# A rebuilt opening for an FFT mixing and MoE kernel: another scratch layout, fewer transfers, later weights

## The chip, the cores and the metric

One core of one Trainium2 chip runs the whole kernel. The time is device time in microseconds (us); a kernel's time is the median of its runs. Engines: PE is TensorE (matmuls; PEld its weight loads), DVE is VectorE, ACT is ScalarE, POOL is GpSimd, SP is SyncE, whose queue (SPq) issues every DMA of this kernel. PEclk is the granted TensorE clock as a share of 2.4 GHz; 0.50 is its other level, 1.2 GHz.

## The reference

```python
X = np.fft.rfft(x, axis=1)                     # x: 8 x 3008 x 256, f32
Yr = Xr @ w_r - Xi @ w_i + b_r
Yi = Xr @ w_i + Xi @ w_r + b_i
Yr, Yi = soft_threshold(Yr, 0.01), soft_threshold(Yi, 0.01)
y = np.fft.irfft(Yr + 1j * Yi, n=3008, axis=1)
out = (np.maximum(y @ w_in, 0) ** 2) @ w_out   # w_in 256 x 2048, w_out 2048 x 256, both f64
```

## The kernel before

The Fourier transform of length 3008 = 47 x 64 is done in two stages each way. Stage A transforms over 47 points, stage B over 64; then come the mix with `w_r` and `w_i`, bias and threshold, stage C (back over 64) and stage D (back over 47). Between the stages the data go through scratch in HBM: `scr1` from A to B, `scr2` from C to D. Frequencies come in 24 rows, worked on as 12 pairs for each batch. Most matmuls take an operand as a high and a low part (`split`, `mm3`: three matmuls for one product).

**The opening** (`start`, an order written out by hand) does all of batch 0 up to the first chunk of tokens, stage A of batch 1, and the weights. `loads` issues the input of batch 0 (`x0`) and the mixing weights. `stage_a(0)` is sixteen matmuls with `tU`, an eviction each (`copy`, in turn on ACT and DVE) and a store into `scr1`. Four weights begin during it, and `tables_start` builds the mixing tables. Then come fifteen rounds over `n`. Round n loads pair n+3 (`bin`) and two pieces of batch 1 (`x1`), does `pair_z(n-2)`, `pair_b(n)` (psb), `pair_mix(n-1)` (psm; the bias comes in as two matmuls of one row, high and low, against `one`), `pair_c(n-3)` and `pair_out` (psc, store to `scr2`), one step of stage A of batch 1 (psa, in rounds 2 to 13), `pair_turn(n-2)`, and one step of every weight under way (`weights`). A weight comes as f64: a load of 0.5 MB into one of four `w64` buffers, `narrow` to f32 (one pass on ACT, four on DVE), a high part by ACT, a low part by GpSimd; for `w_out` four more GpSimd operations on 128 columns. There are eight pieces of `w_in` and eight of `w_out`. After the rounds come `inverse` (loads of `din`, psd, then copy, unfold, high and low of three pieces in turn), the rest of stage A of batch 1, the rest of the weights and `tables_main`.

**The main loop** has 376 rounds of `mm1` (12 matmuls of 512 columns, `ph`), `squares`, `sums`, the split of `g` into `gh` and `gl`, and `mm2` (21 matmuls of 256 columns, `po`), three rounds behind. Stages A to D of the other batches are laid between these by a planner: each job has a round, a place in it and noted costs on ACT and DVE (`PAIR_WORK`, `A_WORK`, `D_WORK`), and `spread` picks the rounds in which these pile up least. `pair_rounds` fixes the pairs' rounds: batch 1 in 1, 3, ... 23. Stage A of batch 2 may begin at round 3. Each engine and each queue works in the order in which its instructions were issued. The first DMA of the loop is a load of `bin`.

Of the kernel before, what the change touches and what calls it, by code (L numbers as in the profile page):

```python
# [75 lines left out]
def tables():  # L76
# [47 lines left out]
    tb0 = tb.reshape(N2 // 4, 2, 2, 2, NR + 1, N2).transpose(0, 2, 3, 1, 4, 5).reshape(P, NR + 1, N2)  # L124
# [25 lines left out]
def fft_mix_moe(ctx: ExitStack, tc: tile.TileContext, xp, xu, w_r, w_i, b_r, b_i,  # L150
# [137 lines left out]

    def start():

        with ExitStack() as own:
# [12 lines left out]
            row = tl("t", name="row")[:1]
            rows = [tl(f"row{k}", (1, 2 * D), F32R) for k in range(2)]
            ones = tl("z", name="ones")[:1, :P]
            one = tMs[:1, 0, :]
# [40 lines left out]
            def tables_start():  # L348
# [8 lines left out]
                split(row, *rows)  # L357
# [15 lines left out]

            def narrow(t, h):


                lo, hi = t[:, :, 0], t[:, :, 1]
                hu = h.bitcast(U32)
                nc.scalar.activation(h, hi.bitcast(F32), AF.Abs)
                yield  # L380
                nc.vector.tensor_scalar(h, h, F_MIN, F_MAX, op0=ALU.max, op1=ALU.min)
                nc.vector.tensor_scalar(hu, hu, 5, 2, op0=ALU.logical_shift_left,
                                        op1=ALU.logical_shift_right)
                nc.vector.scalar_tensor_tensor(hu, lo, 29, hu,
                                               op0=ALU.logical_shift_right, op1=ALU.bitwise_or)
                nc.vector.scalar_tensor_tensor(hu, hi, 0xC0000000, hu,
                                               op0=ALU.bitwise_and, op1=ALU.bitwise_or)
# [23 lines left out]
            def win(c, k):  # L411
                def use(h):
# [5 lines left out]
                    nc.gpsimd.tensor_sub(wi_[1][:, k, s], h, wi_[0][:, k, s].bitcast(F32))  # L418
# [3 lines left out]
            def wout(j):  # L422
                def use(h):
# [9 lines left out]
                    for k in range(2):  # L433
# [3 lines left out]
                    (nc.gpsimd if j < 8 else nc.vector).tensor_sub(wo_[1][j], w7, wo_[0][j].bitcast(F32))  # L437
# [4 lines left out]
                                      (wout(j) for j in range(NU)))  # L442
# [570 lines left out]
```

## Time and profile before

| | us |
|---|---|
| median of 3 runs | 2577.48 |
| lowest and highest | 2576.4, 2577.53 |
| the profiled execution: its own time | 2579.61 |
| its span | 2577.8 |
| TensorE busy in it | 2511.0 (97%) |
| VectorE, ScalarE, GpSimd busy | 2104.9, 1989.6, 48.1 |

The span runs from the first instruction to the last. All of GpSimd's work lies in the first 150 us. Busy time is an average over stages with different limits, so the rows below look at single stretches.

### The profile page before, as it was taken

How to read it: one execution, taken by the hardware profiler on the slowest of the kernel's cores; microseconds unless marked ns; L12 is line 12 of the kernel's file. 1: busy time of each engine (PE TensorE's matmuls, PEld its weight loads, DVE VectorE, ACT ScalarE, POOL GpSimd, SP SyncE). 2: the span in 40 equal slices, each digit the busy share in tenths (PEclk: the TensorE clock that was granted, in tenths of full speed). 3: DMA queues.
4: the chain of work that ended last, by engine and by line, in shares of the span. 5: the costliest groups of instructions: out<-in, count | busy, mean ns of one | idle time of the engine just before them, and what ended most of it. 6: DMA issues, size and time to landing. Idle time of an engine off the chain costs nothing.

```text
span 2577.8 us, 42198 instructions
## 1 busy us (share of the span) xinstructions
PE 2511.0 (97%) x16627; PEld 2262.0 (88%) x16627; DVE 2104.9 (82%) x3155; ACT 1989.6 (77%) x2764; POOL 48.1 (2%) x57
## 2 busy tenths in 40 slices
PE   6979999999999999999999999999999999999999
PEld 3569999999999888999889998899988898899998
DVE  5868888888888888888888888888887888777777
ACT  3668887888788777878877888778877777777776
POOL 1410000000000000000000000000000000000000
PEclk8989999999999999999999999999999999999999
DMA  8622122221221112111122112121121111100000
GB/s 256 187 77 65 49 73 67 79 61 61 80 68 53 56 56 77 56 57 53 56 80 64 53 57 65 60 68 61 45 74 51 41 38 57 36 28 29 21 24 17
DMA packets 113095, 164.61 MB, mean 64 GB/s; under 512 B 9584, under 2 KB 63074, under 8 KB 112706
## 3 DMA queue, kind: packets, MB, share of 16 engines
q1 hardware_dynamic: 112898, 161.91, 20.5%
q8 instruction: 132, 2.16, 0.4%
q14 instruction: 65, 0.53, 0.1%
HBM read 86.90 MB, written 74.97 MB: 63 GB/s over the span
## 4 chain that ended last, share of the span: by engine, by line
PE 80%; DVE 8%; ACT 7%; DMA 3%; issue 2%; SPq 0%; DVEq 0%; ACTq 0%
PE po L906 20%; PE ph L185 10%; PE ph L184 10%; PE ph L186 10%; PE po L910 10%; PE psb L221 3%; PE psd L270 3%; PE psm L184 2%; PE psm L186 2%; PE psm L185 2%; DVE gl L951 2%; ACT g L891 2%; DMA din<-s 1%; ACT gh L946 1%; PE ph L882 1%
## 5 line engine op out<-in xcount | busy, mean ns | idle before, releaser
L951 DVE TENSOR_TENSOR gl<-g,gh 128x1792 fp32r<-128x1792 f32 x376 | 760.2, 2022 | 32.9 <-ACT gh L946 24.5
L891 ACT ACTIVATE g<-ph 128x512 f32<-128x512 f32 x752 | 408.4, 596 | 436.2 <-PE ph L186 305.9
L906 PE MATMUL po<-gh,wo 128*128 128x256 f32 x5264 | 683.8, 281 | 3.1 <-DVE o L923 2.2
L946 ACT CAST gh<-g 128x1792 fp32r<-128x1792 f32 x376 | 637.0, 1694 | 19.8 <-PE po L906 17.2
L906 PEld LDWEIGHTS po<-gh,wo 128*128 128x128 f32 x5264 | 633.3, 188 | 6.5 <-DVE o L923 6.0
L184 PE MATMUL ph<-xt,wi 128*128 128x512 f32 x1373 | 539.0, 393 | 11.9 <-DVE dx L278 9.4
L185 PE MATMUL ph<-xt,wi 128*128 128x512 f32 x1373 | 538.2, 392 | 0.0
L186 PE MATMUL ph<-xt,wi 128*128 128x512 f32 x1373 | 538.1, 392 | 0.0
L897 DVE TENSOR_TENSOR g<-g 128x512 f32<-128x512 f32 x376 | 259.8, 691 | 308.5 <-ACT g L892 306.7
L892 ACT ACTIVATE g<-g 128x1024 f32<-128x1024 f32 x376 | 399.4, 1062 | 12.0
L910 PE MATMUL po<-gl,wo 128*128 128x256 f32 x2632 | 360.5, 277 | 0.0
L910 PEld LDWEIGHTS po<-gl,wo 128*128 128x128 f32 x2632 | 326.8, 188 | 0.0
L184 PEld LDWEIGHTS ph<-xt,wi 128*128 128x128 f32 x1373 | 258.4, 188 | 58.4 <-ACT xt L282 9.5
L186 PEld LDWEIGHTS ph<-xt,wi 128*128 128x128 f32 x1373 | 258.4, 188 | 55.8
L185 PEld LDWEIGHTS ph<-xt,wi 128*128 128x128 f32 x1373 | 258.4, 188 | 44.3
L899 DVE TENSOR_TENSOR g<-g 128x256 f32<-128x256 f32 x376 | 160.0, 425 | 12.9
L898 DVE TENSOR_TENSOR g<-g 128x256 f32<-128x256 f32 x376 | 159.8, 425 | 12.9
L184 PE MATMUL psm<-wm,xh 128*128 128x256 f32 (+1 forms) x552 | 160.9, 291 | 4.4 <-DVE dx L278 3.7
L186 PE MATMUL psm<-wm,xl 128*128 128x256 f32 (+1 forms) x552 | 159.0, 288 | 0.0
L185 PE MATMUL psm<-wm,xh 128*128 128x256 f32 (+1 forms) x552 | 158.9, 288 | 0.0
L221 PEld LDWEIGHTS psb<-tB,bin 128*128 128x128 f32 x768 | 100.6, 194 | 39.0 <-issue 18.5
L270 PEld LDWEIGHTS psd<-tD,din 120*128 120x128 f32 (+1 forms) x832 | 107.2, 191 | 21.8 <-DMA din<-s 11.1
(108 smaller groups left out, 2822.7 us busy)
## 6 DMA issues: line engine op xcount, KB each, us to landing
bin<-s SPq DMA_DIRECT2D x96, 256.0 KB
s<-evc SPq DMA_DIRECT2D x96, 256.0 KB
outT_dram<-o SPq DMA_DIRECT2D x94, 256.0 KB
din<-s SPq DMA_DIRECT2D x96, 240.0 KB
xin<-in_xp_dram SPq DMA_DIRECT2D x72, 240.0 KB
s<-eva SPq DMA_DIRECT2D x72, 240.0 KB
s<-eva SPq DMA_DIRECT2D x22, 192.0 KB
w<-in_moe_w_in_dram SPq DMA_DIRECT2D x8, 512.0 KB
```

Of the source, the lines that this page charges most:

```text
L184: nc.tensor.matmul(out, l0, r0, start=start, stop=False, **kw)
L185: nc.tensor.matmul(out, l0, r1, start=False, stop=False, **kw)
L186: nc.tensor.matmul(out, l1, r0, start=False, stop=stop, **kw)
L221: nc.tensor.matmul(ps[:, k, :, q, :], tv[:, q, k], tB[:, 0:r + 2:r + 1], start=True, stop=True)
L270: nc.tensor.matmul(ps[:, k, part], t[:n, s:s + P], tD[:n, tab + part, :n], start=True, stop=True)
L891: nc.scalar.activation(g[:, 2 * a:2 * a + 2], ph[:, a].rearrange("p (t m) -> p t m", t=2), AF.Relu)
L892: nc.scalar.activation(g[:, 0:4], g[:, 0:4], AF.Square)
L897: nc.vector.tensor_sub(g[:, 4:6], g[:, 1:4:2], g[:, 0:2])
L906: nc.tensor.matmul(out, wo_[k][j][:, s], gh[:, s], start=j == 0 and half == 0 and k == 0, stop=False, skip_group_check=True)
L910: nc.tensor.matmul(out, wo_[0][j][:, s], gl[:, s], start=False, stop=j == NU - 1, skip_group_check=True)
L946: nc.scalar.copy(split_[r - 1][0], hid[r - 1])
L951: nc.vector.tensor_sub(gl, hid.pop(r - 1), gh.bitcast(F32))
```

## The change

- `scr1` is written in another order: one store per step, 48 rows of 4 KB, for both batches of the opening (before, 24 rows in one store for batch 0, two stores for batch 1). The table `t_b0` is permuted to match and serves batch 1 too; `t_b` is loaded into `tB` in the main loop, two rounds after batch 1's last pair.
- `w_r` and `w_i` come as one array and one DMA per half, the two biases as one row pair on partitions 0 and 32. The bias is one matmul over 33 partitions instead of two.
- `x0` is loaded ahead of the mixing weights, in six DMAs instead of seven; no weight begins during stage A of batch 0. Two begin after it and one in each of rounds 0 to 10, thirteen in all. `tables_start` comes after stage A.
- The last three of `w_out` (5, 6, 7) are done in main loop rounds 0, 2 and 5 (`plan_w`), with their four GpSimd operations each.
- Low parts of the weights go from GpSimd to DVE. Evictions of stage C and most of stage A of batch 1 go to ACT.
- Stage A of batch 1 begins at round 7 instead of 2; seven steps are left behind the rounds instead of four, and four of these use the `bin` buffers.
- Matmuls whose result is not used (`idle`): nine before the pairs, two before `inverse`'s matmuls, three after them.
- `inverse` does the three pieces interleaved instead of one by one.
- Main loop: batch 1's pairs in rounds 7, 9, ... 29; stage A of batch 2 from round 12; `e` and `t` of the threshold are one tile `et`, which `plan_w` uses too.

```diff
+LATE = ((5, 0), (6, 2), (7, 5))
-    tb0 = tb.reshape(N2 // 4, 2, 2, 2, NR + 1, N2).transpose(0, 2, 3, 1, 4, 5).reshape(P, NR + 1, N2)
+    tb0 = tb.reshape(N2 // 4, 2, 2, 2, NR + 1, N2).transpose(2, 0, 3, 1, 4, 5).reshape(P, NR + 1, N2)
-    out = {1: [1 + 2 * i for i in range(NPAIR)]}
+    out = {1: [7 + 2 * i for i in range(NPAIR)]}
...
-                load_x0(0, ((0, 2), (2, 4), (4, 8), (8, 12), (12, 16)))
+                load_x0(0, ((0, 2), (2, 4), (4, 8), (8, 16)))
+                load_x0(1, ((0, 8), (8, 16)))
                 for k in range(2):
-                    dma(out=raw[k][:, 1], in_=w_r[k * P:k * P + P, :])
-                    dma(out=raw[k][:, 2], in_=w_i[k * P:k * P + P, :])
-                load_x0(1, ((0, 8), (8, 16)))
-                dma(out=row[:, :D], in_=b_r[None, :])
-                dma(out=row[:, D:], in_=b_i[None, :])
+                    dma(out=raw[k][:, 1:3], in_=w_ri[k * P:k * P + P])
+                dma(out=row, in_=b_ri)
...
-                    nc.gpsimd.tensor_sub(wi_[1][:, k, s], h, wi_[0][:, k, s].bitcast(F32))
+                    (nc.gpsimd if WIL[2 * c + k] else nc.vector).tensor_sub(wi_[1][:, k, s], h, wi_[0][:, k, s].bitcast(F32))
...
-                    (nc.gpsimd if j < 8 else nc.vector).tensor_sub(wo_[1][j], w7, wo_[0][j].bitcast(F32))
+                    (nc.gpsimd if WOL[j] else nc.vector).tensor_sub(wo_[1][j], w7, wo_[0][j].bitcast(F32))
...
-                v = scr1[b].rearrange("r n (c d) -> r (n c) d", c=2)
+                v = scr1[b].rearrange("r n e -> (r n e)").rearrange("(p i e) -> p i e", p=2 * NR, i=nq)
...
-                    tag, n = ("ev", 3) if b else (("bin", 4), ("ev", 3), ("bin", 4), ("ld", 3))[i % 4]
+                    tag, n = (("ev", 3) if i < 12 else ("bin", 4)) if b else (("bin", 4), ("ev", 3), ("bin", 4), ("ld", 3))[i % 4]
                     e = tl(tag, bufs=n, name="eva")[:4 * NR]
-                    copy(i, e, o)
-                    if b == 0:
-                        v0 = scr1[b].rearrange("r n e -> r (n e)")[:, 4 * i * 2 * D:4 * (i + 1) * 2 * D]
-                        nc.sync.dma_start(out=v0.rearrange("r (m e) -> r m e", m=4), in_=e)
-                    for k in range(2 * b):
-                        q = 8 * i + 4 * k
-                        nc.sync.dma_start(out=v[:, q:q + 4], in_=e[:, k * D:k * D + D])
+                    copy(i if b == 0 else EV1[i], e, o)
+                    nc.sync.dma_start(out=v[:, i].rearrange("p (w e) -> p w e", w=2), in_=e)
...
-                for n in range(2):
-                    nc.tensor.matmul(p, one, rows[n], start=n == 0, stop=False)
+                nc.tensor.matmul(p, one, rows, start=True, stop=False)
...
+                for i, t in zip(first, got):
+                    ps[i] = points_d(i, t, pst("psd"))
+                for _ in range(WARM3):
+                    idle()
+                take(first[0])
+                unfold(first[0], ps[first[0]], v[first[0]], xf[first[0]])
+                for i, after in zip(first, first[1:] + [None]):
+                    if after is not None:
+                        take(after)
+                    high_x(pieces(i)[0], xf[i])
+                    if after is not None:
+                        unfold(after, ps[after], v[after], xf[after])
+                    low_x(pieces(i)[0], xf[i])
+
+            TAIL = 2
+            WARM = 9
+            WARM2 = 2
+            WARM3 = 3
+            EV1 = [0] * 10 + [0, 1] * 3
+            EVC = [0] * 12
+            WOL = [0] * 8
+            WIL = [0] * 8
+            X1 = 2, 2, 2, 2, 2, 2, 2, 2, 0, 0, 0, 0, 0, 0, 0
+            A1 = 0, 0, 0, 0, 0, 0, 0, 1, 1, 1, 1, 1, 1, 2, 1
+            WT = 1, 1, 1, 1, 1, 1, 1, 1, 1, 1, 1, 0, 0, 0, 0
...
-                if i == 9:
-                    tables_start()
-                if i in (9,11,13,15):
-                    weights()
-            for i in range(3):
-                load_pair(i)
+            tables_start()
+            load_pair(0)
+            load_pair(1)
             more_loads()
+            load_pair(2)
+            weights()
             weights()
+
+            def idle():
+                nc.tensor.matmul(pst("idle")[:4 * NR], tU, busy, start=True, stop=True)
...
+            for _ in range(WARM):
+                idle()
...
-            nc.sync.dma_start(out=tB, in_=t_b)
-            nc.sync.dma_start(out=bias2[:, 0, :], in_=b_r.partition_broadcast(P))
-            nc.sync.dma_start(out=bias2[:, 1, :], in_=b_i.partition_broadcast(P))
+            nc.sync.dma_start(out=bias2.rearrange("p c e -> p (c e)"), in_=b_ri[0].partition_broadcast(P))
...
+    W_WORK = ((0, .7, 2.3), (1, .8, .8), (2, .6, .7))
...
-            s["e"] = tl("e")
-            add_e(s["e"], *s["p"])
+            s["et"] = tl("et", (P, 2, 512))
+            add_e(s["et"][:, 0], *s["p"])
...
+    at(rounds[NPLAIN - 1][-1] + 2, "load", lambda: nc.sync.dma_start(out=tB, in_=t_b))
...
-    free, begin, b = 2, 3, 2
+    free, begin, b = 2, 12, 2
...
+        at(max(r - 1, 0), "load", load)
+        at(r, "a", magnitude)
+        at(r, "v", narrowed)
+        at(r + 1, "a", high)
+        at(r + 1, "v", low)
+        at(r + 2, "a", high2)
+        at(r + 2, "v", low2)
```

## Rows read from the trace of the kernel before

**Rows 1.** Busy time by stretch: length, busy us of each engine, PEclk, DMA share, GB/s.

```profile
20.00:40.00 20.00, 5.05 (x16) 2.65 (x15) 11.08 (x14) 6.78 (x13) 5.37 (x5) 0.65 0.83 264
...
60.00:80.00 20.00, 20.00 (x84) 13.38 (x83) 16.75 (x33) 11.80 (x23) 3.02 (x2) 1.00 0.97 294
...
400.00:600.00 200.00, 200.00 (x1376) 184.14 (x1375) 171.26 (x262) 164.17 (x230) 0.00 (x0) 1.00 0.22 66
```

**Rows 2.** Timeline of SyncE's queue, opening: start, us, engine, line, operation, names.

```profile
11.03 3.39 SPq L472 DMA_DIRECT2D s<-eva  x4
...
23.48 0.51 SPq L403 DMA_DIRECT2D w<-in_moe_w_in_dram  x1
...
31.48 0.47 SPq L403 DMA_DIRECT2D w<-in_moe_w_in_dram  x1
35.42 1.42 SPq L201 DMA_DIRECT2D bin<-s  x3
```

**Rows 3.** Timeline, the first pairs' matmuls; in brackets idle time before, and releaser.

```profile
38.35 3.76 PE L221 MATMUL psb<-tB,bin 128*128 128x128 f32 x16 [14.95 <-DMA bin<-s]
```

**Rows 4.** Chain that ended last, one pair round and the loop's first: start, us, what.

```profile
96.14 0.86 PE psa L466 x2
97.00 0.89 PE psb L221 x8
97.90 0.67 PE psm L500 x2
...
99.22 0.24 PE psm L186
...
103.28 0.89 PE psb L221 x8
...
148.06 0.43 PE ph L184
```

**Rows 5.** Busy time by stretch, columns as in rows 1.

```profile
42.00:47.00 5.00, 5.00 (x13) 3.56 (x13) 4.86 (x7) 1.90 (x4) 2.07 (x2) 0.55 1.04 321
...
59.40:103.30 43.90, 43.90 (x184) 29.65 (x184) 34.79 (x63) 28.19 (x54) 17.24 (x21) 1.00 0.82 246
...
113.10:126.90 13.80, 7.84 (x13) 2.53 (x12) 11.77 (x16) 6.40 (x13) 6.96 (x10) 0.81 0.25 76
```

**Rows 6.** Timeline, the last pairs.

```profile
112.36 2.24 DVE L382 TENSOR_SCALAR w<-w 128x512 uint32<-128x512 uint32 x1
...
113.13 1.02 PE L525 MATMUL psc<-zh,tM 128*128 128x512 f32 x2
...
126.92 0.37 SPq L209 DMA_DIRECT2D s<-evc  x1
```

**Rows 7.** Timeline, the inverse and the first matmul of the loop.

```profile
129.19 2.38 SPq L261 DMA_DIRECT2D din<-s  x3
...
135.91 1.15 PE L270 MATMUL psd<-tD,din 120*128 120x120 f32 x8 [1.02 <-DMA din<-s]
...
140.69 0.69 DVE L457 COPY eva<-psa 96x512 f32<-96x512 f32 x1 [10.83 <-DMA s<-eva]
...
146.44 0.77 PE L184 MATMUL ph<-xt,wi 128*128 128x512 f32 x1 [9.38 <-DVE dx L278]
```

**Rows 8.** Timeline, the first `ph` matmul of main loop rounds 1 and 3.

```profile
153.12 0.50 PE L184 MATMUL ph<-xt,wi 128*128 128x512 f32 x1 [1.22 <-ACT g L891]
...
162.24 0.50 PE L184 MATMUL ph<-xt,wi 128*128 128x512 f32 x1 [0.97 <-ACT g L891]
```

**Rows 9.** Tile `w`, 0 to 150 us: ns of one, lowest/median/highest; first, last start.

```profile
L382 DVE TENSOR_SCALAR w<-w x16: 426/428/2403, 29.8 to 127.4; 128x512 uint32<-128x512 uint32 x16
L384 DVE SCALAR_TENSOR_TENSOR w<-w,w x16: 691/693/2623, 30.3 to 127.8; 128x512 uint32<-128x512 uint32 x16
...
L428 POOL TENSOR_TENSOR w<-w x8: 453/454/458, 84.5 to 131.7; 128x128 f32<-128x128 f32 x8
```

**Rows 10.** Line 951, the whole span, columns as in rows 9.

```profile
L951 DVE TENSOR_TENSOR gl<-g,gh x376: 2011/2025/2028, 160.5 to 2568.2; 128x1792 fp32r<-128x1792 f32 x188
```

More of the change, by code (lines that the diff above doesn't have):

```diff
@@ L300, in pst @@
                 return pp.tile([P, 512], F32, tag="f", name=name)
+            tl("gap0", (P, 32))
             tM = tl("tM", (P, P))
             tU = tl("tU", (NU1, 4 * NR))
[L304 to L307, printed above, removed]
+            row = tl("t", name="row")[:33]
+            row2 = tl("row2", (33, 2 * D))
+            rows = tl("row1", (33, 2 * D), F32R)
+            ones = tl("z", name="ones")[:33, :P]
+            one = tMs[:33, 0, :]
             nq = N2 // 4
@@ L356, in tables_start @@
                     nc.gpsimd.tensor_sub(m[:, 2], raw[k][:, 2], raw[k][:, 1])
-                split(row, *rows)
+                nc.scalar.copy(rows, row)
+                nc.vector.tensor_sub(row2, row, rows.bitcast(F32))
+                nc.scalar.copy(rows[32:33], row2[32:33])
             def table_a():
@@ L372, in tables_main @@
                 yield
[L374 to L387, printed above, removed]
             def weight(src, use):
@@ L528, in pair_out @@
                 ev = tl("ev", bufs=3, name="evc")
-                copy(i, ev, pc.pop(i))
+                copy(EVC[i], ev, pc.pop(i))
                 store_c(0, i, ev)
@@ L538, in inverse @@
                 yield
[L539 to L552 removed]
+                ps, v, xf = {}, {}, {}
@@ new lines, in take @@
+                def take(i):
+                    v[i] = tl("ld", bufs=3, name="dv")
+                    if pieces(i)[-1][0]:
+                        xf[i] = const.tile([P, 2 * N1 * W], F32, tag="dx", name="dx").rearrange("p (k m) -> p k m", k=2)
+                        kept.append((i, xf[i]))
+                    else:
+                        xf[i] = tl("tz"[first.index(i)], name="dx")[:, :2 * N1 * W].rearrange("p (k m) -> p k m", k=2)
+                    v[i] = v[i][:, :2 * NR * W].rearrange("p (k m) -> p k m", k=2)
+                    nc.scalar.copy(v[i][:, :, :ps[i].shape[3]], ps[i][:, :, 1])
@@ L571, in start @@
                 load_pair(n + 3)
-                load_x1()
-                load_x1()
+                for _ in range(X1[n]):
+                    load_x1()
                 if 0 <= n - 2 < NPAIR:
@@ L579, in start @@
                     pair_mix(n - 1)
+                if n == NPAIR + 2:
+                    for _ in range(A1[n]):
+                        next(a1)
                 if n >= 3:
@@ L582, in start @@
                     pair_out(n - 3)
-                if 2 <= n < NPAIR + 2:
-                    next(a1)
+                if n != NPAIR + 2:
+                    for _ in range(A1[n]):
+                        next(a1)
                 if 0 <= n - 2 < NPAIR:
@@ L822, in fft_mix_moe @@
         note(c * NU + NU + LAG - 2, *SUM_WORK)
+    for _, r in LATE:
+        note(r, *W_WORK)
     def spread(n, lo, hi, work, apart, beside):
@@ L927, in put_together, with plan_w, load, magnitude @@
                               in_=o[k].rearrange("p t m -> p (t m)"))
+    def plan_w(j, r):
+        s = {}
+        def load():
+            s["t"] = tl("et", (P, 512, 2), U32)
+            nc.sync.dma_start(out=s["t"].rearrange("p (f n) w -> p f (n w)", f=2),
+                              in_=w_out.rearrange("(f p) e -> p f e", p=P)[:, 2 * j:2 * j + 2, :].bitcast(U32))
+        def magnitude():
+            s["h"] = tl("z")
+            s["n"] = narrow(s["t"], s["h"])
+            next(s["n"])
+        def narrowed():
+            next(s["n"], None)
+            s["a"] = s["h"].rearrange("p (f e m) -> p f e m", f=2, e=2)
+        def high():
+            for k in range(2):
+                wo_[k].append(ctile(f"wo{k}{j}", [P, NPR, P], F32R))
+            nc.scalar.copy(wo_[0][j][:, 0:3:2], s["a"][:, :, 0])
+            nc.scalar.copy(wo_[0][j][:, 1], s["a"][:, 1, 1])
+        def low():
+            a, c = s["a"], tl("zl", (P, 4, P))
+            s["c"] = c
+            add, sub = nc.gpsimd.tensor_add, nc.gpsimd.tensor_sub
+            add(c[:, 1], a[:, 0, 1], a[:, 1, 1])
+            sub(c[:, 2], a[:, 0, 0], a[:, 0, 1])
+            sub(c[:, 3], c[:, 1], a[:, 0, 0])
+            sub(c[:, 0], a[:, 1, 0], c[:, 3])
+            nc.vector.tensor_sub(wo_[1][j][:, 0:3:2], a[:, :, 0], wo_[0][j][:, 0:3:2].bitcast(F32))
+            nc.vector.tensor_sub(wo_[1][j][:, 1], a[:, 1, 1], wo_[0][j][:, 1].bitcast(F32))
+        def high2():
+            nc.scalar.copy(wo_[0][j][:, 3:], s["c"])
+        def low2():
+            nc.vector.tensor_sub(wo_[1][j][:, 3:], s["c"], wo_[0][j][:, 3:].bitcast(F32))
+        at(max(r - 1, 0), "load", load)
[5 more added lines that the diff above has]
+        at(r + 2, "v", low2)
+    for j, r in LATE:
+        plan_w(j, r)
     hid, split_, pos = {}, {}, {}
```

59 lines of the change are left out of this document (34 added, 25 removed).

## The prediction

> **What bounds the kernel now.** I read the stretches first [rows 1], then the queue of transfers [rows 2], then the chain of waits through the opening [rows 3 to 7], then the first rounds of the main loop [rows 7, 8]. The main loop belongs to TensorE: from 400 to 600 us it is busy for all 200.00 us at full clock, and 2431 of the 2577.8 us lie in the loop. So an edit pays only where TensorE waits, or where it takes work from TensorE. It waits in the opening, which ends when the first `ph` matmul starts, at 146.44 us [rows 7]. The opening has four parts with different limits.
>
> Start, 0 to 38.35 us: the first pair's matmuls wait for the load of `bin`, and that is issued at 35.42, when all sixteen stores of stage A have landed [rows 2, 3]. The transfers move 264 GB/s here with the engines 0.83 busy [rows 1]. Pair rounds, 38.35 to 113.1: TensorE is busy without a gap from 59.4 to 103.3 [rows 5]. One round, from psb to psb, is 97.00 to 103.28, 6.28 us [rows 4]. The first rounds, up to 47 us, ran at the low level of the clock: 0.55 on average from 42 to 47 [rows 5]. Tail, 113.1 to 126.9: the last pairs go through VectorE and ScalarE, while TensorE is busy 7.84 of 13.8 us [rows 5, 6]. Inverse, 126.9 to 146.4: store, load, and a wait of VectorE for a buffer [rows 7].
>
> **The change part by part.** The sum is made on the profiled execution: span 2577.8, its own time 2579.61. The median 2577.48 lies 2.1 below that time and practically on the span, so a saving in the span is taken from the median.
>
> Start. Four weights of 0.52 MB are issued from 23.48 to 31.48 [rows 2], ahead of that load, and none of them is left there. These 2.1 MB at 264 GB/s [rows 1] are 7.9 us, so pairs begin at 30.4. The three small issues saved and the evictions that no longer stand behind the weights' work lie beside the transfers: nothing. Bounds: 5 us, if the stores' issue (0.85 us each, four in 3.39 [rows 2]) binds, to 12.
>
> By the Trainium skill, "DMA: Bandwidth & Descriptors", section "Why a DMA increments its semaphore by 16 and not by 1", a transfer uses the largest number of engines up to 16 that divides the outer sizes of both sides: 12 for 24 rows against 96 partitions, 16 for the new 48 against 96. No row shows the engines one by one. As an estimate by that rule the sixteen stores, 3.15 MB, drain in three quarters of their time, 3.0 us sooner at 264 GB/s; the sum would be 2548.
>
> Warm-up matmuls. Nine `idle` follow stage A, at about 0.86 us each if they run as a `psa` at full clock does [rows 4], so 7.7 us, beside the wait for `bin`. At half clock they would be 15.4 us. If the clock stays up, the sixteen psb matmuls take 1.8 us (twice 0.89 [rows 4]) instead of 3.76 [rows 3], 2.0 saved, and the 5.0 us at clock 0.55 [rows 5] become 2.8, 2.2 saved: 4.2. Bounds 0 to 4.2; I take 4.0.
>
> Pair rounds. One bias matmul of two goes: the pair of them takes 0.67, a later matmul of 512 columns 0.24 [rows 4], the excess being a wait, so I take 0.24 twelve times, 2.9. Stage A of the second batch (`psa`, 0.86 [rows 4]) stood in ten rounds before the last mix and now stands in five: 4.3. That leaves 5.2 us a round without and 6.0 with stage A. Here the cover is thin. A round without stage A loads 1.44 MB (weight 0.52, two x1 0.39, bin 0.26, store 0.26), which at 294 GB/s [rows 1] is 4.9 us. VectorE changes little: eight lows of 0.69 (as a pass with two inputs on the same shape [rows 9]) and five of about 1.05 (half of a 2.02 `gl` [rows 10]) move onto it, 10.8 us, and it loses the stretches in which its passes last 2.24 instead of 0.43 us while GpSimd works [rows 6, 9]. I give back 1.0 for the engines meeting at 5 us: 6.2 saved, bounds 0 to 7.2. All evictions on ScalarE cost nothing while TensorE has 6 us a round.
>
> Tail. Two of VectorE's passes are stretched there, by about 1.8 and 1.9 us (maxima 2403 against 428, 2623 against 693 [rows 9]), and the clock is 0.81 on average [rows 5], about 1.4 us of matmuls. With GpSimd's long lows gone: 5.1 saved. ScalarE now takes three evictions ahead of the last turn, so I expect no more; bounds 2 to 9.
>
> Inverse. Before, 19.5 us from the store's issue at 126.92 to 146.44. What can't go: store to load 2.3 (126.92 to 129.19), load to the third points 6.7 (129.19 to 135.91), 1.15 of matmuls [rows 6, 7]. The third piece's copy, unfold and high are about 1.6 of the 5.1 us that the three took in turn, and the rest now overlaps the loads: 11.8. Saved 7.7. This counts on VectorE's 10.83 us of waiting for `eva` [rows 7] going: seven steps of stage A are left instead of four, but four of them use the free `bin` buffers and `t_b`'s 0.8 MB load is out of the queue ahead of them. If that cover is gone, 5.5 comes back.
>
> Main loop. The same matmuls are done. First round at full clock: twelve matmuls fall from 0.43 to 0.24 [rows 4], 2.3 saved out of the 6.68 us from 146.44 to 153.12 [rows 7, 8]. Against it: rounds 1 and 2 are not bound by TensorE (9.1 us from 153.12 to 162.24 [rows 8], for twice twelve matmuls of 0.24 and a psb or `psd` block, about 7.5) and hid two psb blocks of 0.89 each [rows 4], which now come in rounds that are full, 1.8. The three late weights cost VectorE 3.8 us each by the kernel's own planner (2.3, 0.8, 0.7): nothing if hidden, 11.4 if not. Round 0 hides one, half of the other two shows, 3.8, and 0.7 for the first one's load, behind which the next round's activations queue on ScalarE: 4.5. Net 4.0 lost, bounds -1 and +9. Pairs six rounds later and stage A at round 12 put the same work in other rounds, all with TensorE full as in 400 to 600 [rows 1]: nothing. The later load of `tB` and the merged `et` tile: nothing.
>
> What the row shows of late weights: `narrow`'s passes stretch while GpSimd works [rows 9], and each late weight puts four GpSimd operations of 454 ns into the loop [rows 9]. The Trainium skill, "SBUF — State Buffer", section "Who interferes with whom", says that a VectorE instruction with two SBUF inputs contends with a GpSimd instruction that reads SBUF, and that the one that comes second fully blocks. That speaks against these three weights; the trace agrees for the opening, and no row shows it in the loop.
>
> Sum: 7.9 + 4.0 + 6.2 + 5.1 + 7.7 = 30.9 saved in the opening, which then ends near 115.5; 4.0 lost in the loop. 2577.5 - 30.9 + 4.0 = 2550.6, so 2551.
>
> **The rivals.**
> 1. The opening reaches TensorE's and the transfers' floor: the 7.0 MB ahead of the pairs move at 294 GB/s instead of 264 [rows 1], 2.7 sooner, nothing is given back in the rounds (1.0), and the tail saves 3 more. For: TensorE is the only engine without gaps in the rounds [rows 5]. Against: each engine is near 5 us a round. 2544. By the Trainium skill's rule on the number of engines the first of these would come.
> 2. The rounds stay near 6.28 us because transfers bind: 294 GB/s at 0.97 [rows 1] is already close to all there is, and the new rounds ask for as much in less time. The 6.2 is lost and the tail moves by 1: 2558.
> 3. The late weights block VectorE in rounds 1, 3 and 6: 4 x 0.454 x 3 = 5.5 more [rows 9], so 2556. For: the stretched passes of the opening [rows 6, 9]. Against: four operations of 0.45 are shorter than the lows of 2 us beside which those stretched. By the Trainium skill's rule on the shared interface this is what would happen.
> 4. The change doesn't do what it says: the clock falls before the pairs, or the nine matmuls run at half clock and delay them, and the 4.0 are lost: 2555. For: the clock does fall in the gaps of the tail [rows 5].
> 5. Slower than before: the loop's pace. `et` and the moved `dv` shift working tiles, and if the step of one round grows by 0.1 us, 376 rounds lose 37.6: 2588. It decides from 0.085 us a round. Against: `gl` takes 2011 to 2028 ns over all its buffers [rows 10], so place hardly shows.
>
> **How the numbers follow.** Forecast 0.46 (2546 to 2556), rival 1 0.17, rival 2 0.17, rival 3 0.11, rival 4 0.06, rival 5 0.03. The predicted time is the forecast's. The range runs from 2540, below rival 1, to 2562, where rival 2 meets the weaker tail; it leaves out rival 5 and the outer parts of 1 and 2, together under 0.2. About 0.2%, 5 us, is what a measurement here can tell from no change. Slower by more: 0.03, rival 5. Within 0.2%: 0.03, two of the slow rivals together with a lost inverse. Faster: the rest, 0.94.
>
> **What would show it.** First psb at 29 to 32 us and at full clock (start, warm-up); psb to psb near 5.3 us in the early rounds and 6.0 later (rounds); 8 to 9 us from the last mix to the last `evc` store (tail); some 12 us from there to the first `ph` and no wait of VectorE for `eva` (inverse); first `ph` near 115.5; then 4 us lost by round 8, seen as TensorE waiting on ScalarE or VectorE. If the first `ph` comes before 110 or after 122, the opening is mis-sized; if the rest of the span after it differs from 2431 by over 8 us, the loop is.

## The result, and the profile after

The changed kernel takes 2552.49 us (median of four runs, 2551.18 to 2555.85), the kernel before in runs between them 2577.51. The ratio is 0.9904, with a 95% interval of 0.9887 to 0.9921: 25 us, or 1.0%, faster. The forecast was 2551 with a range of 2540 to 2562. The profiled execution has a span of 2550.4 us and a time of its own of 2552.65.

So the time came out as forecast. The opening did not, and neither did the loop: the opening saved 25.8 us where 30.9 were forecast, and the loop gave back nothing where 4.0 were. The two misses, of about 5 us each, nearly cancel in the sum, which is luck. Most of the experiments are about them. In the spans of the two profiled executions the saving is 27.4 us; the medians show 25.0 because the profiled execution of before took 2.1 us more than its median.

Busy time by stretch, kernel after; the columns are those of [rows 1].

```profile
20.00:40.00 20.00, 18.51 (x66) 9.70 (x65) 7.05 (x9) 8.04 (x15) 4.14 (x4) 1.00 0.86 273
40.00:60.00 20.00, 20.00 (x93) 14.96 (x92) 18.79 (x38) 14.48 (x27) 0.00 (x0) 1.00 1.07 269
60.00:80.00 20.00, 20.00 (x85) 14.03 (x84) 15.49 (x30) 14.51 (x28) 1.23 (x1) 1.00 1.01 313
...
96.07:107.36 11.29, 8.13 (x19) 2.90 (x18) 9.65 (x16) 10.68 (x21) 5.05 (x8) 1.00 0.32 100
107.36:120.68 13.32, 12.25 (x46) 5.89 (x44) 9.61 (x17) 8.22 (x17) 2.17 (x5) 1.00 0.65 213
```

From 20 to 40 us, TensorE was busy for 5.05 us [rows 1]; now it is busy for 18.51, at full clock, and from 40 to 80 it has no gap. The transfers are in use all the time there (1.07 and 1.01), and TensorE still doesn't wait. The last two lines are tail and inverse, which took 13.8 and 19.5 us before [rows 5 to 7].

Chain that ended last, kernel after: start, us, what; two rounds without stage A, two with.

```profile
52.57 0.89 PE psb L222 x8
...
57.72 0.89 PE psb L222 x8
...
68.87 0.89 PE psb L222 x8
...
74.86 0.89 PE psb L222 x8
```

A round is 57.72 - 52.57 = 5.15 us, with stage A 74.86 - 68.87 = 5.99; it was 6.28 [rows 4].

Timeline, kernel after: the start, the inverse, and the first `ph` of main loop rounds 0, 2 and 48.

```profile
18.11 7.63 SPq L473 DMA_DIRECT2D s<-eva  x12
...
22.64 7.89 PE L588 MATMUL idle<-x,tU 96*96 96x512 f32 x18
...
28.18 0.91 SPq L202 DMA_DIRECT2D bin<-s  x2
...
31.14 2.02 PE L222 MATMUL psb<-tB,bin 128*128 128x128 f32 x16 [0.62 <-issue]
...
110.21 2.53 SPq L262 DMA_DIRECT2D din<-s  x3
110.24 1.28 DVE L460 COPY eva<-psa 96x512 f32<-96x512 f32 x2 [1.49 <-PE psa L469]
...
117.83 2.74 PE L588 MATMUL idle<-x,tU 96*96 96x512 f32 x6
118.79 0.39 DVE L279 TENSOR_TENSOR dx<-psd,dv 128x230 f32<-128x230 f32 x1
...
120.68 0.47 PE L185 MATMUL ph<-xt,wi 128*128 128x512 f32 x1
...
129.06 0.50 PE L185 MATMUL ph<-xt,wi 128*128 128x512 f32 x1 [1.18 <-ACT g L927]
...
430.05 0.39 PE L185 MATMUL ph<-xt,wi 128*128 128x512 f32 x1
```

The first pair starts at 31.14 instead of 38.35 [rows 3] and takes 2.02 instead of 3.76; `bin` is issued at 28.18 instead of 35.42. VectorE's wait of 10.83 us for `eva` [rows 7] is now 1.49. The first `ph` comes at 120.68 instead of 146.44, 25.8 sooner. In the kernel before, the first `ph` of rounds 2 and 48 are these rows of its timeline:

```profile
157.32 0.50 PE L184 MATMUL ph<-xt,wi 128*128 128x512 f32 x1 [0.28 <-ACT g L891]
...
458.28 0.39 PE L184 MATMUL ph<-xt,wi 128*128 128x512 f32 x1
```

Rounds 0 to 47 thus took 458.28 - 146.44 = 311.84 us before and 430.05 - 120.68 = 309.37 after: the loop does not lose, it gains 2.5 by then. From round 48 to 71 the two kernels keep step; later their difference wanders, by -2.7 to +1.2 us from one run to another, also between kernels with the same plan. So the cost of something in the loop is read below as the length of rounds 0 to 47 against before's 311.84 ("loop to 48").

### The profile page after: what moved, and what is told of

Read it like the earlier page. It is cut to its first block, busy times and chain, and to the rows that moved or that the text cites. A ratio compares the mean times of both kernels' runs of the same rounds, so it can differ in the third digit from the quotient of the medians.

```text
span 2550.4 us, 42208 instructions
## 1 busy us (share of the span) xinstructions
PE 2511.7 (98%) x16642; PEld 2258.8 (89%) x16642; DVE 2100.8 (82%) x3166; ACT 1994.4 (78%) x2776; POOL 26.8 (1%) x41
## 4 chain that ended last, share of the span: by engine, by line
PE 81%; DVE 8%; ACT 6%; DMA 3%; issue 2%; SPq 0%; DVEq 0%; ACTq 0%
PE po L942 20%; PE ph L186 10%; PE ph L185 10%; PE ph L187 10%; PE po L946 10%; PE psd L271 3%; PE psb L222 3%; PE psm L185 2%; DVE gl L1038 2%; PE psm L187 2%; PE psm L186 2%; ACT g L927 2%; DMA din<-s 2%; ACT gh L1033 1%; DVE g L933 1%
```

## The experiments

All positions in us, one profiled execution each. "psb" is the first pair's start, "psc" the mix that begins the tail (113.13 before [rows 6]), "evc" the issue of the last store ahead of the inverse.

| kernel | `bin` issue | psb | psc | evc | first `ph` | loop to 48 | span | time |
|---|---|---|---|---|---|---|---|---|
| before | 35.42 | 38.35 | 113.13 | 126.92 | 146.44 | 0 | 2577.8 | 2577.51 |
| after | 28.18 | 31.14 | 96.07 | 107.36 | 120.68 | -2.47 | 2550.4 | 2552.49 |
| e1_no_idle | 29.12 | 31.89 | 100.65 | 111.94 | 124.92 | +0.10 | 2554.8 | 2557.09 |
| e2_lows_pool | 27.31 | 30.18 | 95.31 | 107.25 | 120.24 | -2.47 | 2547.4 | 2549.32 |
| e3_no_late | 28.04 | 30.85 | 99.11 | 112.17 | 127.39 | +3.95 | 2560.8 | 2562.83 |
| e4_rows24 | 29.80 | 32.53 | 99.08 | 110.58 | 123.86 | -2.52 | 2550.5 | 2552.79 |
| e5_before_start | 31.64 | 34.70 | 107.2 | 122.3 | 141.46 | +3.16 | 2573.8 | 2575.62 |
| e6_old_plan | 28.26 | 31.09 | 95.78 | 108.64 | 123.84 | +5.05 | 2557.5 | 2559.62 |
| e7_tail | 27.86 | 30.56 | 95.83 | 106.09 | 128.63 | -0.77 | 2556.9 | 2559.57 |
| e8_tail_w3 | 28.66 | 31.54 | 98.03 | 108.25 | 130.83 | -0.27 | 2559.7 | 2561.37 |
| e9_late4 | 28.91 | 32.85 | 96.33 | 107.13 | 118.82 | +0.91 | 2552.3 | 2553.36 |
| e10_late4_ev | 27.69 | 30.56 | 96.07 | 107.04 | 119.42 | +0.83 | 2550.6 | 2552.50 |
| e11_again | 27.72 | 30.54 | 96.7 | 109.19 | 122.87 | -2.55 | 2550.9 | 2553.73 |
| e12_rows24_again | 29.71 | 32.47 | 97.46 | 110.17 | 123.74 | -2.35 | 2551.3 | 2553.60 |

e1 to e6 were run once each, the others four times. after and e11 are the same code: their first `ph` differ by 2.2 us and their spans by 0.5, so a difference of 2 us in the opening is no proof without a row that shows where it arises, while "loop to 48" repeats within 0.2.

**No idle matmuls** (`e1_no_idle`)

```diff
-            WARM = 9
-            WARM2 = 2
-            WARM3 = 3
+            WARM = 0
+            WARM2 = 0
+            WARM3 = 0
```

> All matmuls whose result is not used are taken out (nine, two and three of them), nothing else. Theory (the prediction's): TensorE then stands still from about 22.6 to 31.1 us, its clock falls to the low level, the first pairs run at it, and round n=12's psc comes about 4 us later than 96.07; the three in front of the loop go too, which gives 1.2 us back; the loop's first round may fall to the low level again (2.5 us). First ph about 123.5, time about 2555 to 2558. Rival: the clock does not fall over this gap, or the rounds wait for something else anyway; psc of n=12 stays at 96.1, first ph near 119.4, time about 2551.

2557.09 us, before beside it 2576.11. Timeline of this kernel, then its busy time by stretch:

```profile
31.89 3.44 PE L222 MATMUL psb<-tB,bin 128*128 128x128 f32 x16 [9.14 <-issue]
```

```profile
31.00:33.00 2.00, 1.11 (x5) 1.14 (x6) 0.00 (x0) 0.00 (x0) 0.00 (x0) 0.50 1.02 264
...
36.00:39.00 3.00, 3.00 (x16) 2.50 (x15) 0.00 (x0) 0.00 (x0) 0.00 (x0) 1.00 1.02 374
```

After 9.14 us without work TensorE begins at granted clock 0.50, which is the level of 1.2 GHz; from 36 us it is at 1.00. psc is 4.58 later than in after, but little of this is the clock. Start of psb in some of the rounds, by the timelines:

| kernel | n = 0 | n = 2 | n = 3 | n = 9 | n = 10 | psc |
|---|---|---|---|---|---|---|
| before | 38.35 | 47.58 | 52.97 | 90.57 | 96.84 | 113.13 |
| after | 31.14 | 36.55 | 42.13 | 74.70 | 80.69 | 96.07 |
| e1_no_idle | 31.89 | 38.56 | 43.58 | 77.38 | 85.27 | 100.65 |
| e3_no_late | 30.85 | 39.20 | 43.48 | 76.22 | 83.74 | 99.11 |
| e6_old_plan | 31.09 | 36.34 | 41.72 | 74.29 | 80.40 | 95.78 |
| e8_tail_w3 | 31.54 | 36.75 | 42.42 | 74.99 | 82.65 | 98.03 |

The pairs of e1 begin 0.75 later than those of after. Up to n = 2 they lose 1.3 more, of which 0.7 are left at n = 3. The other 3.1 come at full clock, 1.9 of them between n = 9 and n = 10. There ScalarE waits for a store of `evc` to land, whose buffer it needs, and `zh` comes late. Timeline of e1:

```profile
81.77 0.58 ACT L460 COPY eva<-psa 96x512 f32<-96x512 f32 x1 [4.43 <-DMA s<-evc]
...
83.45 1.13 PE L522 MATMUL psc<-zh,tM 128*128 128x512 f32 x2 [1.64 <-ACT zh L518]
```

ScalarE's wait at this place is 1.90 us in after, where TensorE loses nothing by it, 4.09 in e3 and 3.76 in e8. The clock of e8 was at 1.00 through all its pairs, and it still loses 1.7 there: a fall of the clock is not needed for it. So the nine matmuls are worth about 1 us in the pairs of e1, and the 3.8 between psb and psc must not be read as theirs. Round 0 of the loop begins at the low level as well, and "loop to 48" is 2.6 longer. Forecast were 4.0 and 2.3.

**Lows back on GpSimd** (`e2_lows_pool`)

```diff
-            WOL = [0] * 8
-            WIL = [0] * 8
+            WOL = [1] * 8
+            WIL = [1] * 8
```

> The low parts of the thirteen weights of the opening go back from VectorE to GpSimd, nothing else. Theory (the prediction's): VectorE's passes beside them stretch to some 2.2 to 2.6 us again; the pair rounds hide it behind TensorE, but the tail, from n=12's psc to the last evc store, grows from 11.3 to about 14; first ph near 123.5, time near 2555. Rival: the tail is bound by VectorE's own work, of which each low (1.09 us) is a part; without it the tail shrinks by 1 to 2 us, first ph near 119, time near 2551.

2549.32 us: no slower. Tile `w` through the opening, first of this kernel, then of after; columns as in [rows 9].

```profile
L302 DVE SCALAR_TENSOR_TENSOR w<-w,w x13: 691/1637/2533, 39.9 to 106.1; 128x512 uint32<-128x512 uint32 x13
```

```profile
L302 DVE SCALAR_TENSOR_TENSOR w<-w,w x13: 691/692/828, 41.2 to 106.7; 128x512 uint32<-128x512 uint32 x13
```

The stretched passes are back, with a median of 1637 ns instead of 692, and still the tail is 11.94 us against 11.29 and the first `ph` is at 120.24. Even the 0.65 is not theirs, for the clock differs: in the tail of after it stayed at 1.00, in that of e2 it did not. Busy time of e2:

```profile
100.00:104.00 4.00, 4.00 (x7) 1.10 (x5) 3.85 (x5) 3.42 (x8) 3.31 (x4) 0.57 0.27 87
```

e11, which has the code of after and by chance the same clock there as e2, takes 12.49 for its tail. Moving the lows to VectorE did what the prediction read from [rows 9], but no run shows that it was worth anything in the tail.

**No weights in the loop** (`e3_no_late`), **and also the old plan of the loop** (`e6_old_plan`)

```diff
-LATE = ((5, 0), (6, 2), (7, 5))
+LATE = ()
-            WT = 1, 1, 1, 1, 1, 1, 1, 1, 1, 1, 1, 0, 0, 0, 0
+            WT = 1, 1, 1, 1, 1, 1, 1, 1, 1, 1, 1, 1, 1, 1, 0
```

and in `e6_old_plan` also

```diff
-    out = {1: [7 + 2 * i for i in range(NPAIR)]}
+    out = {1: [1 + 2 * i for i in range(NPAIR)]}
-    free, begin, b = 2, 12, 2
+    free, begin, b = 2, 3, 2
```

> All sixteen weights are done in the opening again (three more begin, in rounds 11, 12 and 13 of the pairs), none in the main loop; the loop's plan keeps the pairs from round 7 and stage A from round 12. Theory A (from the trace of after): late weights cost the loop nothing, since its first rounds wait for ScalarE anyway; the loop from first ph to the end stays within 1 us of 2429.7, and the opening grows by 3 to 8 us, as each of the last pair rounds now carries weight steps on VectorE and some are left behind the inverse. Time 2556 to 2560. Theory B (the prediction's): late weights cost the loop 4.5 us; the loop falls to about 2425, and the time is near 2551.

> The run with all weights in the opening, and the loop's plan of before: batch 1's pairs in rounds 1 to 23, stage A of batch 2 from round 3. Its partner is the run without late weights. The prediction held that pairs in the first rounds use TensorE's waiting there and that moving them out costs 1.8 us: the loop from first ph to the end is then 1.8 us shorter than the partner's. Rival, from the trace of after: those rounds grow by what the pairs add on ScalarE and VectorE, so the two loops agree within 0.7 us.

2562.83 us and 2559.62 us. Up to the loop the two have the same code, and the same granted clock until 31 us. Busy time from 33 to 36 us, first of e3, then of e6:

```profile
33.00:36.00 3.00, 3.00 (x8) 2.05 (x8) 0.33 (x1) 0.00 (x0) 0.00 (x0) 0.50 0.96 292
```

```profile
33.00:36.00 3.00, 3.00 (x14) 2.29 (x13) 0.56 (x1) 0.00 (x0) 0.00 (x0) 1.00 1.00 335
```

In e3 the clock fell just after the pairs began, in e6 it stayed up. At n = 3 (table above) e3 is 1.8 us behind e6, though its pairs began 0.2 sooner, so that one fall costs 2.0 us. At psc it is 3.3 behind (99.11 against 95.78): the rest comes at full clock, between n = 9 and n = 10, in the wait shown under e1. The opening without late weights is therefore read from e6: first `ph` 3.2 us later than in after. Up to 1.2 of it can be the clock, which was at 0.58 from 100 to 104 us in e6 (last section). The loop is read from both: +3.95 and +5.05 against after's -2.47. Most of this is lost ahead of round 2. In e3 ScalarE begins with round 0's activations only after 2.08 us of idling, at 135.62, when VectorE has just finished the last steps of the opening, at 135.53; in e6 the times are 132.06 and 131.98. Timeline of e3:

```profile
135.25 0.28 DVE L180 TENSOR_TENSOR tMs<-tM,tMs 128x128 fp32r<-128x128 f32 x1
...
135.62 1.09 ACT L927 ACTIVATE g<-ph 128x512 f32<-128x512 f32 x2 [2.08 <-issue]
...
136.75 0.80 PE L185 MATMUL ph<-xt,wi 128*128 128x512 f32 x1 [4.62 <-ACT g L927]
```

Why ScalarE waits that long the profile does not say; that the loop's tiles wait for the opening's last ones would fit both kernels, and no run tests it. From the first `ph` of round 2 to that of round 48 before takes 300.96 us, after 300.99, e3 300.21 and e6 301.04. So three weights moved into the loop were worth 2.0 to 3.2 us ahead of it and 6.4 within it (3.95 + 2.47), and behind round 2 they cost 0.8 at most (after against e3). The later pairs and stage A cost nothing either: e6, with the plan of before, is 1.1 us slower by round 48 than e3, not faster. In after the weights' cost and the pairs' gain about cancel.

**The layout of `scr1` back** (`e4_rows24`, `e12_rows24_again`), beside the unchanged kernel (`e11_again`)

```diff
-    ....transpose(2, 0, 3, 1, 4, 5).reshape(P, NR + 1, N2)
+    ....transpose(0, 2, 3, 1, 4, 5).reshape(P, NR + 1, N2)
-                v = scr1[b].rearrange("r n e -> (r n e)").rearrange("(p i e) -> p i e", p=2 * NR, i=nq)
+                v = scr1[b].rearrange("r n e -> r (n e)")
-                    nc.sync.dma_start(out=v[:, i].rearrange("p (w e) -> p w e", w=2), in_=e)
+                    nc.sync.dma_start(out=v[:, 8 * i * D:8 * (i + 1) * D].rearrange("r (m e) -> r m e", m=4), in_=e)
```

> Only the order of scr1 is put back to 24 rows of 8 KB for each store, with the old permutation of t_b0; still one store for each step, and every step at its new place. Theory A: the new layout speeds up the stores; with 24 rows the sixteen stores of batch 0 drain 3 us later, the first psb comes at about 34 instead of 31.14, and the opening ends about 3 us later, near 123.7; time near 2555.5. Theory B: the layout does nothing for the time; first psb stays at 31.1 within 0.5, first ph at 120.7 within 1, time at 2552.5.

> The order of scr1 with 24 rows of 8 KB once more, timed against the partner of this call. In its first run the stores were slower (239 GB/s from 22 to 27 us against 270 to 304 in the others), the first pairs' load was issued at 29.80 against 27.3 to 29.1, and the clock fell before the first psb. Theory A: the new layout is worth 1 to 2 us at the start, and more often than not another 3 us as the later load lets the clock fall; issue of the first bin at 29.5 to 30.5, time 2 to 5 us above the partner. Theory B: that was one run's scatter; issue at 27.5 to 29, time within 1 us of the partner.

> The changed kernel once more, unchanged, as the partner of the other three of this call on the same chip. Its opening should end at 120.2 to 121 where the clock stays up in the first pairs (31 to 39 us), and about 3.3 us later where it falls in the wait between the last unused matmul and the first psb, as in two of the seven runs with this opening's nine unused matmuls so far. Time 2551 to 2556.

`bin` is issued at 29.80 and 29.71 us with 24 rows, and at 27.31 to 29.12 in the ten kernels with 48 rows, 28.18 on average: the layout brings 1.6 us. Timeline of SyncE's queue in e4, the last twelve stores of stage A; those of after are the first row of its timeline above:

```profile
17.47 9.93 SPq L473 DMA_DIRECT2D s<-eva  x12
```

In both kernels these stores are issued back to back, in e4 one every 0.83 us and in after one every 0.65 (the issue alone is 0.74 and 0.55). So twelve of them take 9.93 us instead of 7.63, and `bin` follows 2.4 after the last in both. e12 has 9.93 too, the other kernels with 48 rows 7.6 to 8.0. The last eviction ends at 23.67 in e4 and 23.53 in after, ahead of the last stores, so it isn't the evictions that hold them up; and the very first store, at 11.00 us, already takes 0.74 to issue in e4 and 0.53 in after. What the layout changes, as far as these runs show, is the time that SyncE takes to issue a store. The rate follows from that pace: from 22 to 27 us e4 moves 239 GB/s and after 304, and 192 KB every 0.83 and 0.65 us are 237 and 302. The Trainium skill, "DMA: Bandwidth & Descriptors", section "Why a DMA increments its semaphore by 16 and not by 1", says that a transfer uses the largest number of engines up to 16 that divides the outer sizes of both sides, 12 for 24 rows and 96 partitions, from which the prediction worked out 3.0 us as an estimate. The direction agrees and the size is about half, but no row shows the engines, and the time of issue accounts for the difference without them.

In the time nothing of it is seen: 2553.60 with the old layout (ratio to before 0.9907, 0.9892 to 0.9922), 2553.73 with the new (0.9908, 0.9893 to 0.9923).

**In the kernel before, only the four weights out of stage A** (`e5_before_start`)

```diff
-                if i in (9,11,13,15):
-                    weights()
...
             more_loads()
+            weights()
             weights()
...
-                if n < NPAIR + 1:
+                if n < NPAIR + 3:
```

> The kernel before, with one thing done alone: no weight begins during stage A of batch 0; two begin behind the first pairs' loads and one in each pair round, as many as before in all (the last ones begin later). Theory: the weights' 2.1 MB ahead of the first pairs' load are what made it late; first psb at 30.5 to 32 instead of 38.35. Rival: evictions behind the mixing tables' work and the order of the input loads hold it; first psb at 35 or later. The clock stays low in the first pairs either way (no warm-up matmuls). The weights begun later make the tail longer, so the first ph falls by less than the first psb does, to about 140 to 144, and the time to about 2571 to 2576.

The first pair starts at 34.70 instead of 38.35: 3.65 us, not 7.9. Busy time by stretch, and the timeline of SyncE's queue and of VectorE, of this kernel:

```profile
22.00:27.00 5.00, 0.71 (x2) 0.00 (x0) 4.25 (x5) 2.26 (x5) 1.94 (x2) 1.00 0.61 186
```

```profile
18.06 11.12 SPq L472 DMA_DIRECT2D s<-eva  x12
...
20.54 2.81 DVE L179 TENSOR_TENSOR wm<-raw,wm 128x768 fp32r<-128x768 f32 x2 [2.25 <-ACT wm L178]
...
23.28 1.21 DVE L179 TENSOR_TENSOR row<-row,row 1x512 fp32r<-1x512 f32 x1
...
24.41 1.87 DVE L457 COPY eva<-psa 96x512 f32<-96x512 f32 x3
```

With the weights gone the transfers have room (0.61 in use, 186 GB/s), so they no longer bind. The issue of the stores does: the last twelve take 11.12 us, 9.93 of it at 0.83 each as in e4. In the other 1.2 us SyncE waits for evictions, for VectorE's last three of stage A stand behind the mixing tables (`tables_start`, which the kernel before calls inside stage A) and end at 26.28. In after the tables follow stage A, and the stores are back to back. `bin` follows 2.46 us after the last store, in the kernel before 4.04, with the weights in between.

The time gains nothing that can be seen (2575.62, before beside it 2575.96). The first `ph` comes 5.0 us sooner than in before, though the tail, with the weights that begin later, takes 15.1 instead of 13.8; but 3.2 of it are lost again in the loop's first two rounds.

**No weight steps in the tail** (`e7_tail`), **and two idle matmuls fewer** (`e8_tail_w3`)

```diff
-            TAIL = 2
+            TAIL = 5
-            WP = 1, 1, 1, 1, 1, 1, 1, 1, 1, 1, 1, 1, 1, 1, 1
+            WP = 1, 1, 1, 1, 1, 1, 1, 1, 1, 1, 1, 1, 0, 0, 0
```

and in `e8_tail_w3` also

```diff
-            WARM3 = 3
+            WARM3 = 1
```

> The changed kernel, with the weights' steps taken out of the last three pair rounds (n = 12, 13, 14) and five steps instead of two done behind stage A of batch 1. Theory: in the tail VectorE goes from one pair's threshold through a low and four passes of a weight (about 3.7 us) to the next pair's, and ScalarE likewise; without these steps the tail, from n=12's psc to the last evc store, falls from 11.3 to about 6.5 us, and the steps lie in the wait for the inverse's loads; first ph near 116, time near 2548. Rival: the steps only move in front of the inverse's first unfold, which they now delay; first ph stays at 119.5 to 121 and the time at 2552.

> As the run before in this call, and one instead of three unused matmuls between the inverse's matmuls and the loop. In the changed kernel the three end at about 120.6 us, 0.1 us before the first ph, while the data for it are there at 119.2. Theory: they hold the loop up by about 1.2 us; first ph comes 1.2 us sooner than in the run before, the clock stays up, time 1.2 us lower. Rival: the clock falls before the loop without them, and the loop's first round costs up to 2.5 us more.

2559.57 (ratio 0.9938, 0.9922 to 0.9955) and 2561.37 (0.9943, 0.9929 to 0.9958): both slower than after by 7 us and more. The tail is 10.26 us, only 1.0 shorter. Timeline ahead of the last mix, first of after, then of e7:

```profile
101.63 0.67 ACT L508 ACTIVATE t<-psm,neg 128x512 f32<-128x512 f32 x1
...
102.33 0.69 DVE L509 SCALAR_TENSOR_TENSOR z<-psm,t 128x512 f32<-128x512 f32 x1
102.67 1.04 ACT L460 COPY eva<-psa 96x512 f32<-96x512 f32 x2
103.74 1.02 ACT L518 ACTIVATE zh<-z,sg 64x256 f32<-64x256 f32 x2
104.81 1.12 PE L522 MATMUL psc<-zh,tM 128*128 128x512 f32 x2 [1.40 <-ACT zh L518]
```

```profile
100.17 0.69 DVE L509 SCALAR_TENSOR_TENSOR z<-psm,t 128x512 f32<-128x512 f32 x1 [1.82 <-ACT t L508]
100.64 0.59 ACT L460 COPY evc<-psc 128x512 f32<-128x512 f32 x1 [0.50 <-PE psc L522]
101.54 0.58 ACT L460 COPY eva<-psa 96x512 f32<-96x512 f32 x1 [0.32 <-PE psa L469]
102.40 0.58 ACT L460 COPY eva<-psa 96x512 f32<-96x512 f32 x1 [0.28 <-PE psa L469]
103.01 1.02 ACT L518 ACTIVATE zh<-z,sg 64x256 f32<-64x256 f32 x2
104.08 1.13 PE L522 MATMUL psc<-zh,tM 128*128 128x512 f32 x2 [0.90 <-ACT zh L518]
```

Without the weights VectorE has `z` done 2.2 us sooner (100.86 against 103.02), but ScalarE comes to `zh` at 103.01 all the same: three evictions stand ahead of it. And the weights' steps, now in a row ahead of the inverse, take VectorE from 111.97 to 125.81, with ScalarE waiting 1.78, 2.36 and 2.21 us for GpSimd in three of them. Timeline of e7:

```profile
116.08 0.94 ACT L438 CAST wo<-w 128x896 fp32r<-128x896 f32 x1 [1.78 <-POOL w L434]
...
128.63 0.76 PE L185 MATMUL ph<-xt,wi 128*128 128x512 f32 x1 [9.67 <-DVE dx L279]
```

The wait for `din` hides two such steps, not five. In e8 the fewer idle matmuls change nothing, since VectorE ends last.

**A fourth weight in the loop, one idle matmul** (`e9_late4`), **and evictions moved to VectorE** (`e10_late4_ev`)

```diff
-LATE = ((5, 0), (6, 2), (7, 5))
+LATE = ((4, 0), (5, 2), (6, 4), (7, 6))
-            WARM3 = 3
+            WARM3 = 1
-            WT = 1, 1, 1, 1, 1, 1, 1, 1, 1, 1, 1, 0, 0, 0, 0
+            WT = 1, 1, 1, 1, 1, 1, 1, 1, 1, 1, 0, 0, 0, 0, 0
```

and in `e10_late4_ev` also

```diff
-            EV1 = [0] * 10 + [0, 1] * 3
+            EV1 = [0] * 6 + [1] * 3 + [0] + [0, 1] * 3
```

> A fourth weight of w_out (4) also goes into the main loop (rounds 0, 2, 4 and 6 for 4 to 7), so twelve are left in the opening, and one instead of three unused matmuls stands in front of the loop. Theory: late weights cost the loop nothing (the first rounds wait for ScalarE anyway), so the loop's first 48 rounds take as long as in the changed kernel within 0.5 us; the opening loses one weight's steps on ScalarE and VectorE in the tail, 1 to 3 us, and 1.2 us in front of the loop. First ph 116.5 to 118.5, time 2.5 to 4 us below the partner. Rival: the fourth weight no longer fits beside the first chunk's stage D (rounds 3 to 5) and VectorE delays the loop by 2 us or more; the time is that of the partner within 1 us.

> As the run with four late weights, and the three evictions of stage A of batch 1 that stand on ScalarE ahead of the last turn and of the last evc (steps 6, 7 and 8) go to VectorE. Theory: the tail is bound by ScalarE's order: threshold, evc, two evictions, turn, eviction, evc; without the three evictions (0.58 us each) the tail from n=12's psc to the last evc store is 1 to 1.5 us shorter than in the partner with four late weights. Rival: VectorE's steps of the weights take ScalarE's place and the tail stays within 0.4 us.

2553.36 (0.9906, 0.9892 to 0.9921) and 2552.50 (0.9905, 0.9889 to 0.9922): no different from after. From the issue of `din` to the first `ph` they take 8.85 and 9.65 us; after, e2, e11 and e12 take 10.1 to 10.8, so about 1.2 us of after's inverse is its three idle matmuls (e9 and e10 also have a weight's steps less there). But the fourth weight, with the third one moved from round 5 to 4 and 6, costs the loop 3.4 (+0.91 and +0.83 against -2.47), 2.9 of it behind round 2. The tail with three evictions off ScalarE is 10.97 us, without that edit 10.80: nothing.

## Why the prediction was right, and where it was not

**Start: 7.9 forecast, 7.2 measured, by another cause.** The step said that 2.1 MB at 264 GB/s leave the queue, and that the issues saved and the evictions "that no longer stand behind the weights' work" are worth nothing. What binds is the issue of the stores on SyncE's queue, which the step had only as its lower bound. The weights alone bring 3.65 (e5): the last store is issued 2.2 sooner, as the queue no longer issues weights and waits less between the stores, and `bin` follows it 1.6 sooner. The layout adds 1.6, by a shorter issue. The other 2 us are the 1.2 in which the queue of e5 waits for evictions behind the tables, and a run of stores that begins at 18.06 in e5 and at 17.47 in e4; that is read from the rows of these two, and no run moved the tables alone. The failed step is the division of bytes by a rate, where the rate itself followed from the pace at which transfers were issued. That it came within 0.7 us is luck.

**Warm-up and rounds: right by the rows.** Up to n = 2 the pairs of before take 9.23 us and those of after 5.41, 3.8 less where 4.0 were forecast. Taking the matmuls out of after again costs only 1.3 there (e1), for by the averages of the stretches the clock was back at 1.00 some 3 us after the pairs began in e1, and some 8 us after in before: what a warm-up is worth differs between the runs. Rounds 5.2 and 6.0 forecast, 5.15 and 5.99 measured; no run took the two savings in a round back one by one. From psb to psc 74.78 us became 64.93, 9.85 saved against 10.2. Rival 2 falls for after: 269 and 313 GB/s at a share above 1.0, with TensorE busy for 20.00 of 20 us. But the cover is thin, as the prediction said: in e1, e3 and e8 a store that lands late costs TensorE 1.5 to 1.9 us in one round. Rival 4 happened in part in e3, e4 and e12, where the clock fell at the pairs; in e3 it took 2.0.

**Tail: 5.1 forecast, 2.5 measured.** The failed step is "With GpSimd's long lows gone: 5.1 saved". It added up the stretch of single passes (1.8 and 1.9 us) as if each lay on the path; e2 puts the stretch back and shows no price for it. (The maxima that it read lie ahead of the tail of before; the two passes in and at the start of that tail took 2.24 and 2.47, an excess of 1.8 each, so it is the price that failed, not the size.) The third term, 1.4 for the clock, is borne out by e11: its tail at 0.57 is 1.2 longer than after's at 1.00. No run takes the remaining 1.3 apart. What ends the tail in after is that VectorE's and ScalarE's queues arrive together: VectorE's weight passes give way to `z` at 102.33, and ScalarE's evictions to `zh` at 103.74. e7 relieves the one and e10 the other, for 1.0 and 0. Both in one kernel was not tried.

**Inverse: 7.7 forecast, 6.2 measured.** The cover held: no long wait for `eva`. About 1.2 of the missing 1.5 is a term that the sum lacked, the three idle matmuls: they run from 117.83 to 120.57, and `ph` follows at 120.68, while the last `dx` is done at 119.18. That interleaving the pieces brings the 6.2 rests on the rows before and after; no run took it back alone.

**Loop: 4.0 lost forecast, 1.6 gained measured.** Of its three terms the first is right, the first round at full clock: 2.3 forecast, and 2.5 to 2.6 by after and e1. The other two are not there. The term "half of the other two shows, 3.8, and 0.7": behind round 2 the late weights cost 0.8 at most (after against e3), and by round 48 after, e2, e4, e11 and e12 all stand at -2.4 to -2.6, no more than the clock gives. The term "rounds that are full, 1.8": e6 against e3 shows 1.1 the other way. Both terms charged work on VectorE and ScalarE as if little hid it. The limit is close: a fourth weight costs 3.4.

**Rivals 1, 3 and 5.** Rival 1 lacked the tail. Rival 3, 5.5 us from GpSimd beside VectorE, falls. Tile `zl` and line 1038 of after, columns as in [rows 9]:

```profile
L995 POOL TENSOR_TENSOR zl<-z,zl x3: 462/2123/2129, 132.5 to 160.0; 128x128 f32<-128x128 f32 x3
```

```profile
L1038 DVE TENSOR_TENSOR gl<-g,gh x376: 2012/2024/2273, 132.0 to 2540.3; 128x1792 fp32r<-128x1792 f32 x188
```

Where `gl` (2.02 us) and a GpSimd operation of 0.46 us meet, GpSimd waits: 2123 and 2129 ns, and of 376 `gl` the longest is 0.25 us over the median. The Trainium skill, "SBUF — State Buffer", section "Who interferes with whom", says that the one that comes second is blocked; here that is GpSimd, which is off the path, and so the rule holds without the price. Rival 5 falls too: from round 48 on the rounds of before and after are equal.

## What to carry to other kernels

Before dividing bytes by a rate, ask what sets the rate: here it was the pace at which one queue issued its stores, and both a shorter issue and fewer issues in between paid. A stretched instruction costs its stretch only where no other queue arrives at the same time, so before pricing one, follow the other engine that the same matmul waits for. When a stage ends later in one run than in another, find the row where the time is lost: of 4.58 us that seemed to belong to a missing warm-up, only about 1 arose where it was missing. Steps of preparation that stall a tail can be nearly free in the first rounds of a loop, up to a number that has to be measured: here three cost at most 0.8 us behind round 2, and the fourth 3.4 us.

## What the hardware showed that was not expected

Idle matmuls do not hold the clock in every run. Between the last of them and the first pair lie 0.62 us in after, 1.67 in e2 and 1.90 in e11, where the granted clock stayed at 1.00 (2.4 GHz), and 1.76 in e3, 1.86 in e4 and 3.88 in e12, where it fell to 0.50 in the first 8 us of the pairs. Close gaps went either way.

The same matmuls can meet the low level in the tail, as in e2, e6, e11 and e12. Timeline and busy time by stretch of e11, the same code as after, which has 1.00 through its tail:

```profile
100.35 1.99 PE L522 MATMUL psc<-zh,tM 128*128 128x512 f32 x2 [1.76 <-DVE wo L440]
```

```profile
100.00:104.00 4.00, 3.65 (x5) 1.42 (x6) 3.79 (x7) 3.35 (x7) 2.75 (x4) 0.57 0.18 53
```

The mix takes 1.99 us instead of 1.12, and the tail 12.5 instead of 11.3. And yet the span is only 0.5 us longer: over 376 rounds differences of some 2 us come and go, which is why what the opening gains or loses by 1 or 2 us was not seen in the time.
